# Queries of two tiles in one product, key sums as a column of the key-value product, epsilon on VectorE, the first key weights in two loads, and a new order: four attention layers on one core

## The chip, the core and the metric

The kernel runs on one core of a Trainium2 chip. TensorE (PE in the profile, with its weight loads as PEld), VectorE (DVE), ScalarE (ACT), GpSimd (POOL) and SyncE (SP, which here only issues transfers) each work through a list of instructions in order and wait for one another through semaphores. The metric is the device time of one execution in microseconds (us); lower is better.

## The reference

A sequence of 2048 rows of 512 numbers (bf16) goes through four layers: A, B, A, B with the same weights for both As and both Bs. Each layer normalises its input, attends with 32 heads of 16 columns, multiplies by an output matrix and adds the result to its input. A is linear attention over the whole sequence, B is softmax attention over a causal window of 256 rows.

```python
def _A_ref(x, wqkv, wo):                      # H = 32 heads, Dh = 16
    qkv = (x @ wqkv).reshape(B, S, 3, H, Dh).transpose(2, 0, 3, 1, 4)
    q, k, v = qkv[0], qkv[1], qkv[2]
    phi = lambda t: jnp.where(t > 0, t + 1, jnp.exp(t)) + 1e-6
    pq, pk = phi(q), phi(k)
    kv = jnp.einsum("bhsd,bhse->bhde", pk, v)
    z = jnp.einsum("bhsd->bhd", pk)
    num = jnp.einsum("bhqd,bhde->bhqe", pq, kv)
    den = jnp.einsum("bhqd,bhd->bhq", pq, z)[..., None] + 1e-6
    return (num / den).transpose(0, 2, 1, 3).reshape(B, S, D) @ wo
def _B_ref(x, wqkv, wo):                      # W = 256
    scores = jnp.einsum("bhqd,bhkd->bhqk", q, k) * (Dh ** -0.5)
    p = _softmax(jnp.where(mask[None, None], scores, -1e9), axis=-1)
    return (jnp.einsum("bhqk,bhkd->bhqd", p, v)).transpose(0, 2, 1, 3).reshape(B, S, D) @ wo
x = x + _A_ref(_layernorm(x), A_wqkv, A_wo); x = x + _B_ref(_layernorm(x), B_wqkv, B_wo)
x = x + _A_ref(_layernorm(x), A_wqkv, A_wo); x = x + _B_ref(_layernorm(x), B_wqkv, B_wo)
```

## The kernel before

The 2048 rows are 16 tiles of 128 rows (`T = 16`), and everything stays in the core's memory: the residual `xres`, the weights, and one array `XQ` that holds, for each tile, first the transposed normalised input, then phi of its queries in the same place, later the queries of B.

The program has five parts. `setup` loads inputs and weights. `layer_a_keys` is the first half of the first A: for each tile it normalises (`norm`), transposes the result into `XQ`, makes the keys (`a_k`: four products 512 columns wide, L420, then phi to `pk`), accumulates `g` (L501) over all tiles, and makes the queries of the tile (`a_q`, through `feat`, L434). `barrier` closes an A: from the key-value sums `kv` and the key sums `z` it makes a masked `pqd` (L543) and `zs` (L544) on VectorE, the combined matrix `M` (products L547), then per group G of four tiles the denominators (`den`, L563), their reciprocals (`rec`, L569), and a product (`spread`, L579) that spreads them over the columns, with which phi of the queries is multiplied in place. `middle` runs a B: per tile j it finishes A's output (`a_out`), normalises, makes queries, keys and values, the scores in slices (L676, L712, L792), exponentials on ScalarE (L686, L721, L801, L754), masks, and the products with the values (L822). `middle(2)` also prepares the second A: for each finished tile `norm`, `a_k`, `a_v` (values to `vA`); `barrier(2)` then has `a_kv` and the queries of the second A; `middle(3)` is the second B. I call the parts phase 1 (the first A's sums), the first B, the crossing (the end of the first B, the second A's sums and its barrier), and the second B.

Queries: `feat` makes a tile's queries in 16 products of 128 columns. Each takes a 128x128 block of `wA` as the weights and the tile's 128 columns of `XQ` as what streams through. `phi` is an exponential on ScalarE (L444, `E`), a clip on VectorE (L447, `E1`) and a maximum on VectorE (L451, `phi`), or, for the tiles in `BY_ACT`, an addition on ScalarE (L446, `R`) and a cheaper maximum (L449, `mx`).

Key-value sums of the second A: `a_kv` does per tile four products of 128 columns (L477) into one PSUM bank and four of one column (L480, keys against a column of ones) into another.

The denominators' epsilon of 1e-6 is a first product of `eps` with ones (four of 32x128 per group) ahead of the sixteen that read `zs`.

The order of all instructions does not come from the code's own order. `place` reads it from `TABLE`, a packed string that names, for all operations, their order, the engine of those that two engines can do, and the PSUM bank of every tile; each engine then runs its part of that order, with waits worked out by `synchronise`.

```python
raw = zlib.decompress(b85decode("".join(TABLE)))
order = [ops[raw[2 * k] + 256 * raw[2 * k + 1]] for k in range(n)]
o.eng = ("PE", "ACT", "DVE", "POOL", "SP")[raw[2 * n + o.i]]
```

Seven products `fill` (L277) and nine at the start (L1082) read zeros and only keep TensorE busy until the first data are there.

## Time and profile before

| | |
|---|---|
| median of 3 runs | 409.82 us (409.52 to 409.96) |
| the profiled execution, its own time | 409.61 us |
| its span from the first to the last instruction | 407.9 us |
| granted TensorE clock in it | 1.00 of full speed |
| PE, DVE, ACT, POOL busy in the span | 385.7, 347.8, 349.4, 131.3 us |

A busy engine is not always the one that sets the time. The profile's chain of waits follows the work that ended last back to the start; a table by stage shows which engine has no idle time in a stage; a row of a group gives count, total and mean length of one kind of instruction. TensorE's products overlap, so the length of one (219 ns for 128 columns) is not what it costs in a row of them; that is read from the chain, where runs of products are merged.

### The profile page before, as it was taken

To read this page: it belongs to the slowest core of one execution; us is meant where nothing else is said; L and a number is where in the kernel's file an instruction comes from. 1 tells how busy PE (TensorE), PEld (TensorE's weight loads), DVE (VectorE), ACT (ScalarE), POOL (GpSimd) and SP (SyncE) were. 2 spreads that over 40 slices of the span, in tenths; PEclk is the share of its full clock that TensorE was granted. 3 is DMA by queue.
4 is the path that set the end of the run, shared out by engine and by line. 5 is a ranking of instruction groups with operands and counts; after the bars stand their busy time and mean duration, and the time that the engine had idled before them with its cause. 6 is when DMAs were issued, how large, how long until landed. Compare 5 with 4: busy or idle time off the path is not lost.

```text
span 407.9 us, 17534 instructions
## 1 busy us (share of the span) xinstructions
PE 385.7 (95%) x7667; PEld 261.3 (64%) x7742; DVE 347.8 (85%) x807; ACT 349.4 (86%) x441; POOL 131.3 (32%) x221
## 2 busy tenths in 40 slices
PE   8999999998999999999999999999999989998996
PEld 3754776776575567565667677686756756666664
DVE  7998899999989999888788779998998688856865
ACT  3753679998999999999997258999999999999992
POOL 5668542211430241432512302230305234510340
PEclk9999999999999999999999999999999999999999
DMA  7567024523354444453232000344315534442551
GB/s 251 117 152 232 15 56 107 119 69 81 80 80 106 71 101 104 92 112 91 56 50 62 14 2 2 102 114 107 94 42 106 90 90 104 81 99 70 136 134 54
DMA packets 66788, 37.19 MB, mean 91 GB/s; under 512 B 47640, under 2 KB 62104, under 8 KB 66712
## 3 DMA queue, kind: packets, MB, share of 16 engines
q1 hardware_dynamic: 66320, 35.02, 36.7%
q8 instruction: 61, 1.00, 1.1%
q0 software_dynamic: 384, 1.05, 0.8%
q14 instruction: 15, 0.12, 0.1%
q10 hardware_dynamic: 8, 0.00, 0.0%
HBM read 6.29 MB, written 2.10 MB: 21 GB/s over the span
## 4 chain that ended last, share of the span: by engine, by line
PE 52%; ACT 31%; DVE 9%; issue 4%; DMA 2%; POOL 1%; POOLq 0%; DVEq 0%
ACT pb L686 20%; PE ps L420 18%; PE ps L434 15%; PE ps L822 6%; ACT vp L686 5%; PE ps L676 4%; PE ps L501 3%; ACT pb L801 3%; DVE stats L374 1%; DVE pb L694 1%; DVE xres L604 1%; ACT tE L444 1%; PE ps L792 1%; DMA XQ<-xn 1%; ACT pb L754 1%
## 5 line engine op out<-in xcount | busy, mean ns | idle before, releaser
L686 ACT ACTIVATE pb<-ps 128x1024 bf16<-128x1024 f32 (+2 forms) x216 | 199.0, 1019 | 6.2 <-PE ps L676 5.3
L822 PEld LDWEIGHTS ps<-vB,pb 128*128 128x128 bf16 x2560 | 79.0, 96 | 13.3 <-DVE pb L694 2.8
L822 PE MATMUL ps<-vB,pb 128*128 128x34 bf16 x2560 | 84.9, 177 | 0.9 <-DVE xn L381 0.5
L434 PE MATMUL ps<-xT,wBp 128*128 128x128 bf16 x1024 | 69.3, 219 | 1.3 <-DMA xT<-xn 0.8
L434 PEld LDWEIGHTS ps<-xT,wBp 128*128 128x128 bf16 x1024 | 58.9, 98 | 13.7 <-issue 4.0
L772 POOL TENSOR_SCALAR_AFFINE_SELECT pb<-pb 128x1024 bf16<-128x1024 bf16 x35 | 40.1, 1145 | 84.2 <-DVE pb L694 33.8
L379 POOL TENSOR_SCALAR ve<-mv 128x1 f32<-128x1 f32 x63 | 16.6, 264 | 149.1 <-DVE mv L375 146.9
L444 ACT ACTIVATE tE<-ps 128x512 bf16<-128x512 f32 x64 | 38.1, 606 | 25.3 <-PE ps L420 12.5
L676 PE MATMUL ps<-XQ,kB 32*128 32x256 bf16 (+3 forms) x992 | 48.0, 267 | 2.9 <-ACT vp L686 0.5
L604 DVE TENSOR_TENSOR xres<-ps,xres 128x512 bf16<-128x512 f32 x63 | 43.0, 684 | 7.3 <-PE ps L420 6.8
L420 PE MATMUL ps<-wA,XQ 128*128 128x512 bf16 x174 | 45.8, 379 | 3.4 <-DMA XQ<-xn 0.9
L694 DVE TENSOR_TENSOR pb<-pb,tri 128x512 bf16<-128x512 bf16 (+1 forms) x108 | 43.6, 417 | 2.7 <-ACT pb L686 2.0
L374 DVE BATCH_NORM_STATS2 stats<-xres 128x6 f32<-128x512 bf16 x64 | 43.5, 683 | 2.5 <-DMA xres<-in_A_x_dram 1.9
L380 POOL TENSOR_TENSOR rs<-ve,negh 128x1 f32<-128x1 f32 x64 | 39.5, 616 | 7.7 <-DVE ve L377 2.4
L801 ACT ACTIVATE pb<-ps 128x1024 bf16<-128x1024 f32 x42 | 41.3, 1058 | 0.5 <-PE ps L792 0.4
L434 PE MATMUL ps<-XQ,wA 128*128 128x128 bf16 x512 | 35.5, 219 | 0.2 <-issue 0.2
L434 PEld LDWEIGHTS ps<-XQ,wA 128*128 128x128 bf16 x512 | 30.8, 98 | 6.6 <-DVE xres L604 0.2
L420 PE MATMUL ps<-wBv,xT 128*128 128x512 bf16 x107 | 30.6, 380 | 2.8 <-issue 1.6
L420 PE MATMUL ps<-M,XQ 128*128 128x512 bf16 x112 | 30.5, 380 | 2.0 <-DVE XQ L591 0.5
L420 PE MATMUL ps<-wBo,oT 128*128 128x512 bf16 x109 | 29.8, 380 | 1.8 <-issue 0.8
L676 PEld LDWEIGHTS ps<-XQ,kB 32*128 32x128 bf16 x992 | 14.9, 92 | 25.7 <-ACT pb L686 8.4
L834 DVE RECIPROCAL rc<-ps 128x16 f32<-128x16 f32 x64 | 16.2, 253 | 14.4 <-PE ps L822 13.9
(126 smaller groups left out, 557.4 us busy)
## 6 DMA issues: line engine op xcount, KB each, us to landing
vB<-vS SPq DMA_DIRECT2D x64, 136.0 KB, 2.5
kB<-vp SPq DMA_DIRECT2D x60, 128.0 KB, 2.2
wA<-in_A_wqkv_dram SPq DMA_DIRECT2D x3, 512.0 KB, 4.5
xres<-in_A_x_dram SPq DMA_DIRECT2D x2, 512.0 KB, 5.6
pb<-in_B_wqkv_dram SPq DMA_DIRECT2D x1, 1024.0 KB, 5.5
out_dram<-xres POOLq DMA_DIRECT2D x8, 128.0 KB, 3.2
out_dram<-xres SPq DMA_DIRECT2D x7, 128.0 KB, 3.0
xres<-in_A_x_dram SPq DMA_DIRECT2D x3, 256.0 KB, 4.8
```

What stands on the lines that cost most here:

```text
L374: self.on("DVE", "stats", lambda e: e.bn_stats(K.stats[:, t, :], x()), key, dve(512), rd=rd, wr=[("stats", t)], **held)
L380: self.pow = self.on("POOL", "pow", lambda e: e.tensor_tensor(K.rs[:, t, :], K.ve[:, t, :], K.negh[:], ALU.pow), key + 0.03, (640, 690), r ...
L420: m = e.matmul(K.ps(ps), lhs(c), rhs(c), start=c == 0 and not whole, stop=c == 3)
L434: m = e.matmul(K.ps(ps)[:, f * P:(f + 1) * P], w(c, f), xT(c), start=c == 0, stop=c == 3)
L444: self.on("ACT", "E", lambda e: e.activation(K.tE[:, s, :], K.ps(ps), ACT.Exp, bias=0.0), key, act(512), wr=[("tE", s)], ps=[ps])
L604: self.on("DVE", "res", lambda e: e.tensor_tensor(K.xres[:, t, :], K.ps(po), K.xres[:, t, :], ALU.add), key, dve(512), rd=[("xres", t)], w ...
L676: m = e.matmul(K.ps(ps[gq])[:, ns * i:ns * i + ns], K.kB[rows, j % 4, 2 * f + b, :, :], K.XQ[rows, f, q:q + ns], start=True, stop=True, ti ...
L686: return e.activation(out(2 * h, 2, ns), i, ACT.Exp, bias=0.0, scale=0.25)
L694: return e.tensor_tensor(x, x, K.tri[:, 0, sh:64].unsqueeze(1).unsqueeze(1).to_broadcast([P, 4, n, 64 - sh]), ALU.mult)
L772: return e.affine_select(out=x, in_=x, compare_op=ALU.is_ge, fill=0.0, base=-2, pattern=[[0, 16], [-2, 64]], channel_multiplier=1)
L801: return e.activation(far(h), i, ACT.Exp, bias=0.0, scale=0.25)
L822: m = e.matmul(K.ps(ps)[:, 34 * u:34 * u + 34], K.P((b // 2) % rp)[:, gq, f, o:o + P], K.vB[:, (b // 2) % 4, b % 2, r, :], start=i == 0, s ...
```

## The change

Four edits and a new table.

**Queries in pairs.** `a_q` is called for two tiles at a time. Each product streams the 256 columns of both tiles past one 128x128 block of weights, so 16 products of 256 columns stand where 32 of 128 stood. The pair fills two PSUM banks, each with half of the features of both tiles. Since phi of the queries overwrites `XQ` of both tiles, the first write waits for all 16 products of the pair (`after=held`).

**Key sums as a 129th column.** Values `vA` now have rows of 516 numbers: four blocks of 128 values, each followed by a one (written by the new `unit`: one memset on VectorE, one on GpSimd). `a_kv` streams 129 columns against the keys, so the last column is the sum of the keys; the one-column products are gone. The operands are swapped, so `barrier(2)` masks two halves on VectorE (`kvm`, `zs`, each twice), transposes on TensorE and copies to `pqd` on VectorE or ScalarE. Phase 1 still has its own sums `z`.

**Epsilon on VectorE.** For groups 1 to 3 the epsilon products are gone, and an addition of 1e-6 to 128x128 numbers in PSUM (`de`) stands ahead of the reciprocal.

**First key weights in two loads.** `wAk` is loaded as two transfers of 256 KB, and each half of a key product waits for its own.

```diff
-        seq += [xs(0, 1), w("wAk", "wA", "A_wqkv", 512, 1024), xs(1, 2), ...
+        def wk(h):
+            return ("wAk%d" % h, lambda e: e.dma_start(K.wA[:, 2 * h:2 * h + 2, 512:1024], ...), 262144, [("wAk", h)])
+        seq += [xs(0, 1), wk(0), wk(1), xs(1, 2), ...
...
-    def a_q(self, t, key, near=False):
-        ps = self.feat("q", t, lambda c, f: K.wA[:, c, f * P:(f + 1) * P], lambda c: K.XQ[:, c, t * P:(t + 1) * P], [("XQ", t), ("wAq",)], key)
-        self.phi(ps, lambda: K.XQ[:, :, t * P:(t + 1) * P], [("XQ", t)], key + 0.1, 1, near)
+    def a_q(self, u, keys, near):
+        own = [("XQ", 2 * u), ("XQ", 2 * u + 1)]
+        wide = lambda t: slice(256 * (t // 2), 256 * (t // 2) + 256)
+        for t in (2 * u, 2 * u + 1):
+            ps = Tile(1, K.cls)
+            xT = lambda c, t=t: K.XQ[:, c, wide(t)]
+            for h in range(2):
+                def put(e, h=h, t=t, ps=ps, xT=xT):
+                    f = 2 * (t % 2) + h
+                    for c in range(4):
+                        m = e.matmul(K.ps(ps)[:, 256 * h:256 * h + 256], K.wA[:, c, f * P:(f + 1) * P], xT(c), start=c == 0, stop=c == 3)
+                self.pe("q", put, keys[t % 2] - 0.001 * h, 4, 256, rd=own + [("wAq",)], ps=[ps])
+        held = [o for x in own for o in self.g.r[x]]
+        for t in (2 * u, 2 * u + 1):
+            d = t % 2
+            out = lambda t=t: K.XQ[:, 2 * (t % 2):2 * (t % 2) + 2, wide(t)]
+            wr = [("XQ2", 2 * u), ("XQ2", 2 * u + 1)] if d else own
+            self.phi(tiles[d], out, wr, keys[d] + 0.1, 1, t in near, after=held)
...
+    def unit(self, a, b, more, key):
+        x = lambda: K.vA[:, a:b, :].rearrange("p t (f x) -> p t f x", f=4)[:, :, :, P:P + 1]
+        self.g.add("unit", {"POOL": (300, 360), "DVE": dve(4 * (b - a))}, lambda e, eng: e.memset(x(), 1.0), ...)
...
-                e.matmul(K.ps(kv)[:, fs], K.vA[:, t, fs], K.pk[:, t, fs], ...)
-                m = e.matmul(K.ps(z)[:, f:f + 1], K.pk[:, t, fs], K.ones[:, 0:1], ...)
+                m = e.matmul(K.ps((kv, z)[f // 2])[:, 129 * (f % 2):129 * (f % 2) + 129], K.pk[:, t, f * P:(f + 1) * P], K.vA[:, t, 129 * f:129 * f + 129], ...)
...
+        if late:
+            for h, x in enumerate((kv, z)):
+                self.on("DVE", "kvm", lambda e, h=h, two=two: e.tensor_tensor(K.oT[:, 0, 2 * h:2 * h + 2, :], two()[:, :, 0:P], ...
+                self.on("DVE", "zs", lambda e, h=h, two=two: e.tensor_tensor(K.zs[:, 2 * h:2 * h + 2, :], ...
+            self.transpose("T", lambda: K.oT[:, 0, :, :].rearrange("p f n -> p (f n)"), lambda: K.pqd[:], ..., True)
...
-                for i in range(5):
+                for i in range(1 if G else 0, 5):
...
+            if G:
+                self.on("DVE", "de", lambda e, ps=ps: e.tensor_scalar(K.ps(ps)[:, 0:P], K.ps(ps)[:, 0:P], 1e-6, None, op0=ALU.add), k + 0.05, dve(128), ps=[ps])
...
 TABLE = (
-    r"c-qZ(1Jo_cu5~4qq^h=U+qP}nwr$(CZQHhO+qTZ@{=U8ccX95y=VH9^_Zq8_N@kLoRMzScDx?aflnSfDsqiX-LPaW}N~992Br2l%>b|&dE|SWsvZ<shvij^k",
+    r"c-qZb1DGz$uB}v(O4V%Jwr$(CZQHhO+qP}nwr#!s|JnP!bI-ZH=eytQnVzn$N>;6`q%(idC>2(PQ{hzz6;g##p;ZKhidAeCN5xg~R73^J1Oy4-fJiE<%BJEg",
...
+ROW = D + 4
...
-            sb("vp", [2 * T, D]); ...
+            sb("vp", [T * (ROW + D)]); ...
```

The new table changes the order on every engine. Two places of it matter below; before and after print the lines of their own source (L434 is L483 after, L547 is L581, L563 is L597, L686 is L723).

The first place is TensorE in the crossing, from the last key-value products to `M`. Before:

```order
L477 MATMUL ps<-vp 128x128 x4
L480 MATMUL ps<-ones,vp 128x1 x4
L434 MATMUL ps<-XQ,wA 128x128 x8
L563 MATMUL ps<-ones,eps 32x128 x4
L563 MATMUL ps<-XQ,zs 32x128 x16
L434 MATMUL ps<-XQ,wA 128x128 x8
L547 MATMUL ps<-wAo,pqd 128x512 x3
L579 MATMUL ps<-rec,spread 128x128 x16
```

And now:

```order
L506 MATMUL ps<-vp 128x129 x24
L483 MATMUL ps<-XQ,wA 128x256 x8
L398 MATMUL ps<-ident,oT 128x128 x4
L597 MATMUL ps<-ones,eps 32x128 x4
L597 MATMUL ps<-XQ,zs 32x128 x16
L581 MATMUL ps<-wAo,pqd 128x512 x2
L483 MATMUL ps<-XQ,wA 128x256 x4
L581 MATMUL ps<-wAo,pqd 128x512
L616 MATMUL ps<-rec,spread 128x128 x16
```

The transposes of the masked sums (L398, `ident,oT`) are new, and no queries stand between the denominators and `M` any more.

The second place is ScalarE at the start of the first B, where the exponentials of the scores (L721 and L686 before, L758 and L723 after) begin. L444 and L447 are the `E` of phi, L407 and L410 copies out of PSUM, L627 and L664 the copy of keys. Before:

```order
L627 ACTIVATE vp<-ps 128x512
L721 ACTIVATE pb<-ps 128x8x128 x4
L407 ACTIVATE XQ<-ps 128x4x128
L444 ACTIVATE tE<-ps 128x512
L627 ACTIVATE vp<-ps 128x512
L686 ACTIVATE pb<-ps 128x2x2x256 x10
L444 ACTIVATE tE<-ps 128x512
L627 ACTIVATE vp<-ps 128x512
L686 ACTIVATE pb<-ps 128x2x2x256 x8
```

And now:

```order
L664 ACTIVATE vp<-ps 128x512
L758 ACTIVATE pb<-ps 128x8x128 x4
L410 ACTIVATE XQ<-ps 128x4x128
L447 ACTIVATE tE<-ps 128x512
L664 ACTIVATE vp<-ps 128x512
L723 ACTIVATE pb<-ps 128x2x2x256 x18
```

An `E` and a copy of keys have left the run of exponentials; the eighteen now follow one another.

More of the change, by code (lines that the diff above doesn't have):

```diff
@@ L437, in feat, with phi @@
         return ps
-    def phi(self, ps, out, wr, key, ring, near=False):
+    def phi(self, ps, out, wr, key, ring, near=False, after=()):
         K = self
@@ L450, in phi @@
         else:
-            self.on("DVE", "phi", lambda e: e.scalar_tensor_tensor(out(), view(K.ps(ps)), 1.0 + 1e-6, view(K.tE[:, s, :]), ALU.add, ALU.max), key + 0.02, dve(512), rd=[("tE", s)], wr=wr, ps=[ps])
+            self.on("DVE", "phi", lambda e: e.scalar_tensor_tensor(out(), view(K.ps(ps)), 1.0 + 1e-6, view(K.tE[:, s, :]), ALU.add, ALU.max), key + 0.02, dve(512), rd=[("tE", s)], wr=wr, ps=[ps], after=after)
     def a_k(self, t, key):
@@ L475, in put @@
             for f in range(4):
-                fs = slice(f * P, (f + 1) * P)
-                e.matmul(K.ps(kv)[:, fs], K.vA[:, t, fs], K.pk[:, t, fs], start=t == 0 and f == 0, stop=t == T - 1, skip_group_check=True)
-            for f in range(4):
-                fs = slice(f * P, (f + 1) * P)
-                m = e.matmul(K.ps(z)[:, f:f + 1], K.pk[:, t, fs], K.ones[:, 0:1], start=t == 0 and f == 0, stop=t == T - 1, skip_group_check=True)
+                m = e.matmul(K.ps((kv, z)[f // 2])[:, 129 * (f % 2):129 * (f % 2) + 129], K.pk[:, t, f * P:(f + 1) * P], K.vA[:, t, 129 * f:129 * f + 129], start=t == 0 and f % 2 == 0, stop=t == T - 1, skip_group_check=True)
             return m
-        self.pe("kv", put, key, 4, 128, occ=330, rd=[("pk", t), ("vA", t), ("ones",)], ps=[kv, z], after=self.closing)
+        self.pe("kv", put, key, 4, 129, rd=[("pk", t), ("vA", t)], ps=[kv, z], after=self.closing)
     def layer_a_keys(self, ph, base):
@@ L907, in middle @@
             self.on("POOL", "zero", lambda e, i=i: e.memset(K.vA[:].rearrange("p t d -> p (t d)")[:, 1152 * i:1152 * i + 1152], 0.0), base - 5, (1080, 1140), wr=self.room[i] + [("vA", 2)])
+        if not last:
+            self.unit(LATE, T, [], base)
         for t in range(min(3, T)):
```

163 lines of the change are left out of this document (89 added, 74 removed).

## The prediction

> **What bounds the kernel now.** I first read the table by stage, cut at the first key products (7 us), the first scores (60), the end of the first B's exponentials (216), the last tile's arrival in the second A (232), the second B's first scores (257) and its last exponentials (397). Columns: stretch, its length, then busy time and instruction count of PE, PEld, DVE, ACT and POOL.
>
> ```profile
> 7.00:60.00 53.00, 52.28 (x569) 32.52 (x576) 49.37 (x122) 30.94 (x54) 33.36 (x65) 1.00 0.48 128
> 60.00:216.00 156.00, 148.66 (x3088) 100.16 (x3121) 140.40 (x325) 151.15 (x177) 44.28 (x73) 1.00 0.40 89
> 216.00:232.00 16.00, 14.93 (x312) 11.31 (x300) 13.03 (x32) 8.49 (x15) 5.32 (x7) 1.00 0.17 36
> 232.00:257.00 25.00, 24.48 (x389) 18.54 (x395) 21.19 (x50) 17.00 (x30) 4.05 (x10) 1.00 0.01 2
> 257.00:397.00 140.00, 132.65 (x3162) 91.40 (x3181) 114.04 (x258) 137.05 (x160) 40.71 (x54) 1.00 0.42 99
> ```
>
> Phase 1 belongs to TensorE (52.28 of 53), the two Bs to ScalarE (151.15 of 156 and 137.05 of 140), and in the crossing TensorE is full again while ScalarE is idle for 7.5 and 8.0 us. The chain of waits (start, us, what) has these pieces:
>
> ```profile
> 8.15 1.73 PE ps L420 x8
> ...
> 10.10 1.79 PE ps L434 x32
> ...
> 228.03 4.15 DMA XQ<-xn
> ...
> 233.57 0.24 PE ps L477 x4
> 233.82 0.08 PE ps L480 x4
> 233.90 0.24 PE ps L477 x4
> ...
> 240.53 0.39 PE ps L563 x20
> ...
> 241.53 0.59 PE ps L547 x2
> ```
>
> From 7 to 60 us it stays on TensorE; the waits of that engine there, all of them, are
>
> ```profile
> PE ps L420 <- issue: 0.2, 1, 0.2
> PE ps L434 <- issue: 0.2, 1, 0.2
> ```
>
> so phase 1 lasts as long as its products. Outside the Bs and phase 1 the one visible stall is the load at 228.03.
>
> **Phase 1: -0.3 us (0 to -0.6).** The order of the change has the same products ahead of the first scores as before, 176 query products of 128 columns having become 88 of 256. Thirty-two of 128 take 1.79 us, 55.9 ns each; eight of 512 take 1.73 us, 216 ns each. On the line between, 256 columns cost 109 ns, against 112 for two of 128. So the pairs save 88 x 2.5 ns = 0.2 us here, and 256 x 2.5 = 0.6 us in the whole kernel; the bounds are nothing (112) and half of a 512 (108). One group's four epsilon products (a fifth of 0.39 us, 0.08) go too.
>
> The Trainium skill, "TensorE: Matmul & The Clock Gate", section on the back-to-back issue gap, says otherwise: in a sustained stream of weight loads and products, 128 columns cost about 81 ns each, not the isolated 56. The trace does not agree: its stream of 32 runs at 56 with a weight load for each. By the page 512 products would be 41.5 us and halving their number would be worth many times the 0.6; I keep that as a rival below, priced from rows.
>
> The split key load I cost at nothing: TensorE starts its first keys at 6.82 us, and the copy they read ended at 6.70:
>
> ```profile
> 2.27 0.47 SPq L297 DMA_DIRECT2D wA<-in_A_wqkv_dram  x1
> ...
> 6.10 0.60 ACT L402 ACTIVATE XQ<-ps 128x512 bf16<-128x512 bf16 x1 [2.80 <-PE ps L395]
> ...
> 6.82 0.13 PEld L420 LDWEIGHTS ps<-wA,XQ 128*128 128x128 bf16 x2
> ```
>
> The copy hides the weights. The extra issue on SyncE's queue (0.47 us) delays the rows and query weights behind it by that much; TensorE has key products of three tiles (8 x 216 ns and more) ahead of the queries, which cover it. Without that cover it would cost the 0.5 once.
>
> **First B: -1.6 us (0 to -2.0).** This is the new order's part, not one of the four edits. I counted ScalarE's list from the first exponentials of this B to its last: 185 instructions where 188 stood, one `E`, one copy of queries and one copy of keys less. Rows (busy us, mean ns, idle before):
>
> ```profile
> L444 ACT ACTIVATE tE<-ps 128x512 bf16<-128x512 f32 x64 | 38.1, 606 | 25.3 <-PE ps L420 12.5 <-PE ps L434 6.8 <-DVE vp L451 3.8
> ...
> L627 ACT ACTIVATE vp<-ps 128x512 bf16<-128x512 f32 x5 | 4.0, 792 | 0.0
> ```
>
> With the copy of queries as long as the `E` of the same 128x512, 0.606 + 0.606 + 0.792 = 2.0 us go out of the engine that has only 4.85 us of idle time in 156. TensorE's list there is 0.8 us shorter (two products of 512 columns, the epsilons of two groups, 2.5 ns for each of 72 wide products), VectorE's as long as before, with 15.6 us idle. If ScalarE alone decided, all 2.0 would come; if TensorE, 0.8; if the data arrive no earlier, nothing. I take 1.6, since ScalarE has the least room.
>
> **Crossing: -0.4 us (-1.7 to +1.1).** Gone are the one-column products: after the wait that ends at 232.2, eleven tiles of `a_kv` stand on the chain, and row 233.82 shows that one tile's take 0.08 us, 0.10 until the next tile's run at full pace (five tiles more stand ahead of the wait, where they are free): -1.1 us. Streaming 129 columns instead of 128 is under 1 ns a product. The pairs save 44 x 2.5 ns = 0.1.
>
> Added is a longer way from the sums to `M`. The rows for VectorE's part, and two stretches in which VectorE is full (third busy time):
>
> ```profile
> L835 DVE TENSOR_TENSOR o<-ps,rc 128x256 bf16<-128x256 f32 x64 | 26.7, 419 | 1.5
> ...
> L543 DVE TENSOR_TENSOR pqd<-ps,bmask 128x512 bf16<-128x512 f32 x2 | 1.4, 687 | 0.0
> ...
> L544 DVE TENSOR_TENSOR zs<-hot,ps 128x128 bf16<-128x128 bf16 x2 | 0.6, 288 | 1.1 <-PE ps L480 0.6 <-PE ps L524 0.5
> ...
> L377 DVE TENSOR_SCALAR ve<-mv 128x1 f32<-128x1 f32 x1 | 0.2, 154 | 0.0
> ```
>
> ```profile
> 240.00:250.00 10.00, 9.89 (x144) 7.07 (x144) 9.78 (x24) 7.76 (x15) 0.79 (x2) 1.00 0.02 3
> 250.00:260.00 10.00, 9.90 (x183) 7.33 (x182) 9.94 (x24) 9.84 (x15) 2.48 (x6) 1.00 0.15 43
> ```
>
> Before, `zs` and the mask take 0.29 + 0.69. Now two masks of 256 (0.42 each, by L835) and two `zs` of 64 columns (between the 0.15 of one column and the 0.29 of 128; I take 0.22), 1.28 us; then the copy of the transposed sums, between the 0.42 of 256 and the 0.69 of 512 columns from PSUM, taken at the low end, 0.42, since it reads bf16. On TensorE the four transposes take 0.24, as four products of 128 columns do (row 233.57), and wait for both masks: 0.84 plus a hop after the last key-value product, behind eight query products of 0.87, so hardly at all. The denominators, 0.39, run while the copy is made; `M` then follows about 1.85 us after the last key-value product, against 1.46 before (the products ahead of row 240.53 are 8 x 56 ns, so the sums end at 240.07, and `M` starts at 241.53), where sixteen query products fill the time. TensorE thus loses 0.24 + 0.39 = 0.6 us, behind which all queries and the output of the first tiles queue.
>
> `de` is not in the trace: between 0.15 (one column, L377) and 0.29 (128 columns, two operands), taken as 0.22, six times in the kernel. Two of them and the copy fall from 240 on, where VectorE has 0.3 us idle in 20; I count 0.2 of the 0.86 on the path, since TensorE, not VectorE, is the chain there. Sum: -1.1 - 0.1 + 0.6 + 0.2 = -0.4. With VectorE as the bound the additions count whole and the savings not: +1.1. Without the loss of TensorE and with the one-column products of all sixteen tiles on the path: -1.7. ScalarE gets 2.6 us more in the crossing, in 15.5 idle; the ones of `unit` are on queues with room.
>
> **Second B: +0.5 us (0 to +0.8).** The list of exponentials is almost word for word the old one, with one more copy of keys on ScalarE, 0.79 us where 3 are idle in 140. Three `de` meet 26 us idle on VectorE. The end of the kernel has the same products and additions; ten stores instead of eight go over GpSimd's queue, where only the last row's wait counts.
>
> **Sum.** -0.3 - 1.6 - 0.4 + 0.5 = -1.8 us. The profiled execution took 409.61 around its span of 407.9, 0.21 under the median; on the median 409.82 it gives **408.0 us**. My own range for it: all terms at their good ends -4.3, or 405.5; at their bad ends I go up to 409.0.
>
> **Rivals.**
> *Pairs that make phi late: slower.* In the first B a query's `phi` on VectorE could start after its tile's 16 products, 0.89 us; now it waits for the pair's, 1.74, 0.87 later, and masks and the residual queue behind it on VectorE, then the scores' banks, then ScalarE. The first B has 72 of the wide products, 4.5 pairs: 4.5 x 0.87 = 3.9 us if none is hidden. It decides once VectorE reaches the phi less than 0.87 us after the tile's products. For it: VectorE is 90% busy and in order. Against it: 15.6 us idle there. With the other terms: 409.8 - 1.8 + 3.9 = 411.9 us.
> *Shifted rows: slower.* Tiles of `vA` now lie 1032 bytes apart, and eleven transposing loads of phase 1 read them:
>
> ```profile
> XQ<-vp SPq DMA_TRANSPOSE x11, 2.5
> ```
>
> If each took a quarter longer, 0.6 us, and TensorE waited for each, it would be 11 x 0.6 = 6.9; TensorE waited for none before, so I give 2 to 4 of it, 411 us. The Trainium skill, "DMA: Bandwidth & Descriptors", section on how a descriptor splits into AXI transactions, has a transfer that does not start on a 256-byte boundary cost an extra transaction (five for four here); no run here shows it.
> *A new balance that brings nothing.* VectorE is above 90% in the first B and full from 240 to 260, and the work on it grows by 6 x 0.22 + 0.3 + 0.42 = 2 us: the gains of the other two go into its queue, 409.4 us.
> *Weight loads that count.* Were the query products worth their mean busy time,
>
> ```profile
> L434 PE MATMUL ps<-XQ,wA 128*128 128x128 bf16 x512 | 35.5, 219 | 0.2 <-issue 0.2
> ```
>
> that is 35.5 / 512 = 69 ns, the pairs would save 512 x 69 - 256 x 109 = 7.6 us, 402.2 us. Against it: the merged row at 56.
>
> **How the numbers follow.** My forecast has 0.57, the late phi 0.16, the shifted rows 0.05, no change 0.16, the counting weight loads 0.06. What differs by more than 0.2% (0.8 us) from the median can be told from no change here. Faster: forecast and weight loads, 0.63; the same: 0.16; slower: 0.21. The range takes in the good ends and a little of the weight loads, and of the slower cases about half: 404.6 to 411.0.
>
> **What would show it.** In the changed profile: sixteen wide query products in a row last 1.74 us (much less: weight loads count); the first scores start at 59.2 instead of 59.45; ScalarE's busy time in the first B is 2 us less and its stretch as much shorter; `M` starts 1.8 to 1.9 us after the last key-value product; the second B is as long as before plus half a microsecond. Long waits of VectorE's phi for L483, or of TensorE for the transposing loads before 60 us, would prove me wrong, as would idle time of ScalarE within either B.

## The result and the profile after

| | before | changed | ratio (95% interval) |
|---|---|---|---|
| median of 11 runs each, us | 409.74 | 411.29 | 1.0034 (1.0017 to 1.0050) |
| lowest and highest run, us | 409.02, 410.16 | 409.76, 412.84 | |
| profiled execution, us (its span) | 409.61 (407.9) | 412.54 (410.8) | |

The change made the kernel 0.34% slower, about 1.4 us; 408.0 us were predicted, with a range of 404.6 to 411.0. The first B's row of the table by stage, changed kernel, first profile (stretch, length, busy time and count of PE, PEld, DVE, ACT, POOL, granted clock, DMA share, GB/s):

```profile
60.00:216.00 156.00, 147.01 (x2954) 97.53 (x2985) 139.28 (x324) 148.25 (x171) 43.37 (x71) 1.00 0.39 88
```

In the 156 us that held 177 instructions of ScalarE before, 171 now fit: the first B is longer, not shorter. (The 2954 products beside 2985 weight loads are no edit: 31 products left no record, as the second experiment shows for the kernel before.) From the changed kernel's chain of waits (start, us, what), rows at its start, in phase 1 and in the first B:

```profile
5.27 1.28 PE ps L277 x3
...
8.02 0.86 PE ps L423 x4
...
11.05 1.75 PE ps L483 x16
...
134.32 4.05 DMA XQ<-xn
...
138.47 0.41 DVE xn L384
138.88 0.61 DVE XQ L410
...
139.54 0.43 PE ps L616 x16
```

The sixteen wide products take the 1.75 us that I priced. The first key products start at 8.02 (7.01 before), since three fill products still took 1.28 us, 427 ns each, where they took 216 ns each before. In the two traces the first record of the full granted clock is at 7.18 us (changed) and 4.99 us (before). At 134.32 a new wait stands on the chain: the normed rows of the second A have one buffer, VectorE may not write it before the transposing load of the tile before has read it, and a copy of queries, a product and the next factors queue behind. It looked like the cause. By e2 and e6 below it was not: without it the loss stays.

**One table for all runs.** To place gains and losses I counted the 312 exponentials in ScalarE's timeline and split each profiled execution at three of them: number 0 (first scores of the first B), 150 (near its end) and 156 (the second B's first), then the last and the span's end. Worked out from the traces, in us:

```
kernel                          to no. 0  first B  crossing  second B  end   span
before                             59.90   159.18     37.16    142.70  8.93  407.9
before, second profile             59.91   158.95     37.05    142.70  8.93  407.5
changed                            60.46   161.38     35.27    144.11  9.60  410.8
changed, second profile            59.67   160.30     35.27    143.50  9.60  408.3
e1  old code, new order            60.39   160.08     36.77    143.05  9.59  409.9
e2  two xn buffers                 60.47   160.50     35.27    143.86  9.59  409.7
e3  no 129th column                59.74   159.83     36.65    142.84  9.58  408.6
e4  narrow products                61.09   160.96     35.35    145.06  9.60  412.1
e7  before, more ScalarE           60.65   160.97     37.31    142.84  8.93  410.7
e8  before, more TensorE           60.45   162.35     36.74    143.05  8.94  411.5
e9  before, 129th column           59.60   165.69     37.36    142.88  8.94  414.5
e10 mended order                   60.01   161.72     35.27    144.82  9.25  411.1
e11 before, 129th, ones split      59.84   159.26     37.36    144.05  8.98  409.5
e12 before, less ScalarE           60.55   158.56     37.07    142.29  8.93  407.4
e13 old code, new first half       59.88   161.20     38.96    142.68  9.42  412.1
e14 old code, new second half      60.13   158.95     40.59    143.64  9.58  412.9
e15 changed, old end               59.54   161.42     35.27    143.81  8.94  409.0
e16 e15 with two xn buffers        60.22   160.46     35.27    144.33  8.94  409.2
```

The first column varies from 59.5 to 60.7 with either code (e4 apart): what the first profile lost there is not the change's. The second profiles of the two kernels differ by 0.8 us of span, and the stretches add up to it: -0.24 + 1.35 - 1.78 + 0.80 + 0.67 = 0.80.

### The profile page after: what moved, and what is told of

Its sections match the earlier page's. It is cut to its first block, busy times and chain, and to the rows that moved or that the text cites. A ratio compares the mean times of both kernels' runs of the same rounds, so it can differ in the third digit from the quotient of the medians.

```text
span 410.8 us, 16888 instructions
## 1 busy us (share of the span) xinstructions
PE 385.4 (94%) x7327; PEld 256.1 (62%) x7402; DVE 345.7 (84%) x814; ACT 351.1 (85%) x444; POOL 132.5 (32%) x224
## 4 chain that ended last, share of the span: by engine, by line
PE 67%; ACT 13%; DVE 11%; issue 5%; DMA 4%; POOL 1%; POOLq 0%; DVEq 0%
PE ps L423 22%; PE ps L437 11%; PE ps L859 11%; ACT pb L723 8%; PE ps L713 6%; PE ps L483 6%; PE ps L527 3%; ACT vp L723 3%; DMA XQ<-xn 2%; DMA oT<-o 2%; DVE xres L641 2%; PE ps L829 2%; DVE XQ L628 1%; DVE stats L377 1%; PE ps L1124 1%
## 5 line engine op out<-in xcount | busy, mean ns | idle before, releaser
L723 ACT ACTIVATE pb<-ps 128x1024 bf16<-128x1024 f32 (+2 forms) x216 | 199.5, 1024 | 8.3 <-PE ps L713 7.7
L447 ACT ACTIVATE tE<-ps 128x512 bf16<-128x512 f32 x64 | 37.9, 604 | 18.9 <-PE ps L423 9.9
L731 DVE TENSOR_TENSOR pb<-pb,tri 128x512 bf16<-128x512 bf16 (+1 forms) x108 | 42.3, 402 | 3.7 <-ACT pb L723 3.6
L383 POOL TENSOR_TENSOR rs<-ve,negh 128x1 f32<-128x1 f32 x64 | 38.2, 596 | 7.5 <-DVE ve L380 2.3
L483 PE MATMUL ps<-XQ,wA 128*128 128x256 bf16 x256 | 33.5, 273 | 0.9 <-ACT pb L723 0.4
L423 PE MATMUL ps<-wBo,oT 128*128 128x512 bf16 x103 | 28.2, 380 | 3.9 <-DMA oT<-o 1.3
L483 PEld LDWEIGHTS ps<-XQ,wA 128*128 128x128 bf16 x256 | 23.6, 98 | 8.2 <-ACT pb L723 0.9
```

The lines of the kernel that those rows point to most:

```text
L383: self.pow = self.on("POOL", "pow", lambda e: e.tensor_tensor(K.rs[:, t, :], K.ve[:, t, :], K.negh[:], ALU.pow), key + 0.03, (640, 690), r ...
L423: m = e.matmul(K.ps(ps), lhs(c), rhs(c), start=c == 0 and not whole, stop=c == 3)
L483: m = e.matmul(K.ps(ps)[:, 256 * h:256 * h + 256], K.wA[:, c, f * P:(f + 1) * P], xT(c), start=c == 0, stop=c == 3)
L723: return e.activation(out(2 * h, 2, ns), i, ACT.Exp, bias=0.0, scale=0.25)
L731: return e.tensor_tensor(x, x, K.tri[:, 0, sh:64].unsqueeze(1).unsqueeze(1).to_broadcast([P, 4, n, 64 - sh]), ALU.mult)
```

## The experiments

The theories: **A**, the new order loses the time and the four edits are worth about their price, in its narrow form by single new waits; **B**, pairs of queries come late; **C**, the waits only show where work piles up; **D**, TensorE and not ScalarE bounds the Bs. Ratios are to the kernel before, run on the same chip.

### The order alone: e1, old code in the new order

```diff
-    TABLE of before (order, engines, banks)
+    TABLE of the changed kernel, without the 14 operations that only it has
```

> The kernel before, instruction for instruction (query products of one tile, key sums by one-column products, epsilon by TensorE, one load of key weights), put in the order, on the engines and in the PSUM banks of the changed kernel's table. Theory A (the new order loses the time, the four edits are worth about what I priced them at): 411 to 412 us, with VectorE waiting 1 to 2 us for the transposing load ahead of a second A's xn between 130 and 150 us, and the exponential number 78 about 1.3 us later than in the kernel before. Rival B (the queries of two tiles do it: a pair's phi comes late): no loss in this kernel, 408 to 409.8 us, and no such wait.

Measured: 411.75 us, 1.0062 (1.0043 to 1.0082). The order alone loses 2.5 us by the ratio; the edits in it (1.0034) give about 1.1 back, though the two intervals overlap. B falls: this kernel has no pairs, and in e6 VectorE's phi of queries waits only 0.3 us for the products of a pair in the whole first B. The wait that I had named is not in e1's profile (number 78 comes 0.8 us later than in e5, but 72 was already 0.7 late, 0.5 of it from the start), so A holds and its narrow form is in doubt. The split load and the epsilon on VectorE have no run of their own.

### What bounds the Bs: e5, e7, e8, e12

The prediction rests on ScalarE's being the fuller engine. The first row of the page for before, then the same row of its second profile:

```profile
PE 385.7 (95%) x7667; PEld 261.3 (64%) x7742; DVE 347.8 (85%) x807; ACT 349.4 (86%) x441; POOL 131.3 (32%) x221
```

```profile
PE 394.2 (97%) x7742; PEld 262.0 (64%) x7742; DVE 347.3 (85%) x807; ACT 349.2 (86%) x441; POOL 131.4 (32%) x221
```

e5 is the kernel before, unchanged.

> The kernel before, unchanged, for a second profile: the first one has 7667 products beside 7742 weight loads of TensorE, so 75 products, all of 512 columns, left no record. Theory D (TensorE bounds the whole kernel, and the idle time that I read for it in the two Bs is made of missing records): with all records TensorE's busy time is 394 to 396 us instead of 385.7, and in the first B (60 to 216 us) it is idle for under 3 us, less than ScalarE's 4.9. The reading of the prediction (ScalarE bounds the Bs): 7 us idle of TensorE in the first B stay.

With all records TensorE is busy for 394.2 us, 8.5 more, and by the table by stage of this second profile idle for 2.6 us of the first B, less than ScalarE (4.7):

```profile
60.00:216.00 156.00, 153.43 (x3125) 100.43 (x3123) 140.63 (x325) 151.27 (x177) 44.34 (x73) 1.00 0.41 89
```

The page had said so: each product has its weight load, and 7667 stand beside 7742. D's numbers hold (TensorE's busy time has modelled ends in it, so its 2.6 us of idle time are an estimate). Both engines are nearly full there, and the next three runs load or relieve one of them.

```diff
 e7:  e.activation(K.tE[:, s, :], K.ps(ps), Exp)
+     ahead of it: e.activation(K.pqd half, K.ps(ps)[:, 0:256], Exp)        (13 tiles)
 e8:  for c in (2 * h, 2 * h + 1): e.matmul(K.ps(ps), lhs(c), rhs(c), ...)
+     ahead of it, twice: e.matmul(K.ps(ps), lhs(0), rhs(0), start, stop)    (11 tiles)
-e12: e.activation(K.tE[:, s, :], K.ps(ps), Exp)
+e12: e.activation(K.tE[:, s, 0:64], K.ps(ps)[:, 0:64], Exp)                 (8 tiles)
```

> The kernel before with twelve more activations of 128x256 on ScalarE in the first B (each exponent of a second A key tile, 2 to 13, is taken once more of half its columns, into the free buffer pqd): 12 x 0.38 = 4.6 us of work, each right ahead of the E that VectorE waits for. ScalarE bounds the Bs (the prediction's reading, 4.9 us idle in 156): 3 us or more slower. Theory D (TensorE bounds them): 0 to 1.5 us slower.

> The kernel before with 22 more products of 512 columns on TensorE in the first B (two ahead of the value products of tiles 1 to 11, overwritten by them): 22 x 0.216 = 4.75 us of work. ScalarE bounds the Bs (7.3 us idle of TensorE in 156): 0 to 2 us slower. Theory D: 4 to 5 us slower.

> The kernel before with less work on ScalarE in the first B: the exponents of eight key tiles of the second A (2 to 9) are taken of 64 columns instead of 512, the other columns keep what stood there. From 0.60 us for 512 columns and 0.38 for 256 about 0.21 for 64, so 8 x 0.39 = 3.1 us less work; TensorE and VectorE have the same work. The prediction's term (1.6 of 2.0 us saved on ScalarE come out): 407.2 us. The rate of the run with more work on ScalarE (2.2 us for 4.6): 408.2 us. If TensorE sets the first B: 409.3 to 409.7.

The totals of the three profiles, e7, e8 and e12:

```profile
PE 395.8 (96%) x7742; PEld 262.2 (64%) x7742; DVE 347.8 (85%) x807; ACT 352.5 (86%) x454; POOL 131.5 (32%) x221
```

```profile
PE 399.5 (97%) x7764; PEld 264.3 (64%) x7764; DVE 348.0 (85%) x807; ACT 350.3 (85%) x441; POOL 131.2 (32%) x221
```

```profile
PE 394.7 (97%) x7742; PEld 262.2 (64%) x7742; DVE 347.1 (85%) x807; ACT 346.7 (85%) x441; POOL 131.4 (32%) x221
```

Measured: e7 1.0053 (1.0037 to 1.0068), so 3.3 us more of ScalarE cost 2.2; e8 1.0087 (1.0067 to 1.0107), 5.3 us more of TensorE cost 3.6; e12 0.9983 (0.9973 to 0.9992), 2.5 us less of ScalarE give 0.7. The edit of e7 takes thirteen tiles, not the twelve of the expectation (454 instructions of ScalarE where 441 stood). Work added to either engine costs two thirds of itself, but work taken from ScalarE returned a quarter: by the intervals 0.46 to 0.84 of what was added in e7 and 0.13 to 0.44 of what was taken in e12. The quarter may be too much: e12's profile has 0.4 us of its gain in the first B and 0.4 in the second, where nothing was edited. That TensorE holds the rest fits these numbers; VectorE, busy for 140.63 of the 156 us, was never loaded or relieved by itself, so its part isn't known. This is the number that the prediction lacked. Neither reading was right as it stood: ScalarE does not bound the first B alone, and neither does TensorE.

### The changed kernel again: e6

> The changed kernel, unchanged, for a second profile and more times. If the 1.1 us that its first profile lost between the exponentials number 72 and 78 (VectorE waiting for a transposing load that took 4.05 us) were the order's doing, they are lost here too; if that was one slow load, the exponential number 78 comes 0.2 to 0.7 us later than in the kernel before, and the profiled time is 410 to 411.5 us. Under both, the parts that four kernels in this order lose alike stay: 1.4 us gained between number 12 and 18, 1.8 lost between 24 and 42, 2.1 lost between 180 and 186.

Measured over ten runs: 411.51 us, 1.0036 (1.0020 to 1.0051), its profiled execution 410.07. The loss of 1.1 us between the exponentials 72 and 78 is not in it; e13 and e15 have it (1.0 and 1.4 us) and e4 a part (0.6), e1, e3 and e10 don't (0.1 to 0.2). There a load is just in time or just not. The gain between 12 and 24 and the loss between 24 and 42 and between 180 and 186 are in every profile that has the new order there.

### The waits: e2, e10, e16

```diff
 e2, e16:
-    self.norm(j, k, 3, ...)            # the one xn buffer
+    self.norm(j, k, 3 + j % 2, ...)    # slot 4 is pqd
```

> The changed kernel with one edit: the normed rows of the second A alternate between their one buffer and the buffer pqd, which is free from 60 to 240 us, so that VectorE's next xn needn't wait until the transposing load of the tile before has read the only buffer. Order, engines and banks as they were. Theory A in its narrow form (this wait starts the loss of the first B): VectorE's waits for that load are gone, the exponential number 78 comes 1.0 to 1.3 us earlier, and the kernel takes 409.3 to 410.3 us. Rival C (TensorE and VectorE are full there, the wait only shows where work piles up): the wait goes, but the scores come no earlier, 411 us and more.

Measured: 411.14 us, 1.0042 (1.0027 to 1.0057). The wait is gone and so is the jump at 72 to 78 (which e6 lacks too, with one buffer), but not the loss: that is what C expects. I then mended four places at which the chain of the second profile leaves TensorE's work. This is the worst of them (e6's chain of waits):

```profile
203.18 1.83 PE ps L423 x8
205.01 0.36 PE ps L713 x8
...
205.39 1.95 ACT pb L723 x2
...
207.39 1.05 PE ps L483 x8
208.44 0.33 PE ps L713 x8
```

Query products wait until ScalarE has read two tiles of scores, since their bank held scores, and the next scores stand behind them. In e10 they go behind those scores; the other moves, in TensorE's order:

```diff
 L713 MATMUL ps<-XQ,kB 128x256 x8
-L423 MATMUL ps<-wBo,oT 128x512 x2
 L423 MATMUL ps<-wA,XQ 128x512 x4
+L423 MATMUL ps<-wBo,oT 128x512 x2
 L829 MATMUL ps<-XQ,kB 128x64 x32
...
 L713 MATMUL ps<-XQ,kB 128x256 x8
-L423 MATMUL ps<-wA,XQ 128x512 x4
 L859 MATMUL ps<-vB,pb 128x34 x48
+L423 MATMUL ps<-wA,XQ 128x512 x4
...
-L483 MATMUL ps<-XQ,wA 128x256 x8
 L713 MATMUL ps<-XQ,kB 128x256 x8
+L483 MATMUL ps<-XQ,wA 128x256 x8
...
+L423 MATMUL ps<-wBo,oT 128x512 x2
 L859 MATMUL ps<-vB,pb 128x34 x24
 L713 MATMUL ps<-XQ,kB 128x64 x8
-L423 MATMUL ps<-wBo,oT 128x512 x2
```

> The changed kernel with four places of its order put as they were before, or past a wait, nothing else: the query products that wait for a bank of scores go behind the next scores (with the first half's phi), two output products of the first B go behind the key products of A instead of waiting for their transposing load, key products that wait for their load go behind value products of B, and the last but two output products go ahead of the last scores, their load and bank with them. Theory A (the order's loss is made of such places, at which TensorE waits for a bank or a load while ScalarE runs dry): 0.5 to 0.8 us at the exponentials 132 to 144, 0.2 to 0.5 at each of the two loads, 0.4 to 0.6 behind the last exponential, 1.2 to 2 us in all: 409.5 to 410.3 us. If the loss is spread over the order (TensorE's work moved out of stretches that ScalarE bounds into stretches that TensorE bounds): the waits go, but most of the time stays, 411 us.

Measured: 412.85 us, 1.0070 (1.0049 to 1.0090), slower than the changed kernel. Beside e6, the two moves at the loads gained 0.5 us (exponentials 102 to 108) and lost 1.0 behind it (108 to 114), the one at the scores lost 0.8 (138 to 144), and the last made the end 0.3 shorter and the last exponential 0.7 later. Gains at the places that were mended came with losses elsewhere. A's narrow form falls, at least for these four places together; no run moves one of them alone. e16 comes from e15 (below):

> The changed kernel with the old end (from some 294 us on) and with the second xn buffer of the second A (pqd). If the wait for the one buffer explains the spread: the exponential number 78 is no more than 0.3 us behind the number 72 in its distance to the kernel before, and the times are 409.3 to 410.3 us with their median at 409.8, no slower than before. If it is one of several loads that come late now and then: 410.3 to 410.7 us, as with one buffer, and a spread of 1.5 us or more.

Measured: 410.76 us, 1.0028 (1.0011 to 1.0045), from 409.84 to 413.76. The second buffer doesn't narrow the spread, so this wait does not explain it.

### The 129th column: e3, e9, e11

```diff
 e3, in the changed kernel:
-    m = e.matmul(K.ps((kv, z)[f // 2])[:, 129 columns], pk, vA[:, t, 129 * f:129 * f + 129], ...)
+    e.matmul(K.ps(kv)[:, fs], K.vA[:, t, fs], K.pk[:, t, fs], ...)
+    m = e.matmul(K.ps(z)[:, f:f + 1], K.pk[:, t, fs], K.ones[:, 0:1], ...)
 e9, in the kernel before, in its own order: the reverse, with the ones and the transposes
 e11:
-    self.unit(0, LATE, ...)
+    self.unit(0, 2, ...)               # ahead of the values of tile 0
+    self.unit(2, LATE, ...)            # ahead of those of tile 4
```

> The changed kernel with the key sums of the second A by one-column products again (64 of them, ones as the moving operand), and so without the ones in the rows, without the transposes of the sums and their copy, with one mask and one zs; all else in the new order. By my terms the 129th column is worth -1.1 + 0.6 + 0.1 (the copy's part) = -0.4 us, so 411.5 to 412.0 us and M about 1.5 us after the last key-value product; if the longer way from the sums to M costs more than it saves, 410.3 to 411.0 us.

> The kernel before, in its own order, with one of the four edits: the key sums of the second A as the 129th column (rows of 516 elements, the ones, two masks and two zs, the transposes of the sums and their copy). Three kernels with the 129th column take 35.2 to 35.3 us from the first B's last exponentials to the second B's first, two without it 36.6 and 36.8, so the edit is worth 1.4 us of the crossing: 408.3 us (407.9 to 408.7), faster than both kernels. By my own price for the edit alone (-1.1 + 0.6 + 0.1 = -0.4 us) it would be 409.3 us.

> The kernel before, in its own order, with the 129th column, as in the run that took 417.5 us, but the ones for the last five tiles of values are written in two pieces, each right ahead of the values that need it. In that run one memset waited 2.4 us on VectorE for the last copy of keys out of the same rows (which landed at 202.8 us), with the copies of other values behind it, and TensorE and ScalarE behind those: 6.6 us between the exponentials 126 and 138. If that wait was all of it, no stretch of the first B is longer than before and the crossing shows what the 129th column is worth: 408.3 us if 1.4, 409.3 if 0.4.

Measured: e3 412.33 us, 1.0079 (1.0050 to 1.0108), with a crossing of 36.65 against 35.27; e9 417.55, 1.0188 (1.0166 to 1.0210); e11 411.23, 1.0027 (1.0012 to 1.0043), with a crossing of 37.36 against 37.05. So in single profiles the column is worth 1.4 us of the crossing in the new order and costs 0.3 in the old one. The chains of waits of the crossing say why, first before (second profile), then the changed kernel (e6):

```profile
227.81 4.04 DMA XQ<-xn
...
231.90 1.04 PE ps L420 x4
```

```profile
232.12 1.18 PE ps L506 x20
233.30 0.86 PE ps L423 x4
234.16 0.22 PE ps L398 x4
234.39 2.59 PE ps L423 x12
236.98 1.42 PE ps L506 x24
238.40 0.87 PE ps L483 x8
239.27 0.39 PE ps L398 x4
...
239.68 0.44 DVE pqd L405
...
240.16 0.61 PE ps L581 x2
```

Before, TensorE waits in the crossing for the last tiles' load, and the one-column products of the tiles ahead of it are free. In the new order nothing is waited for, every product counts, and the longer way to `M` (1.76 us from the last key-value product, 238.40, to 240.16) is filled with eight query products and the transposes.

e9 shows what a wait in the wrong place costs. Its chain of waits:

```profile
200.61 2.17 DMA kB<-vp
...
202.90 0.09 DVE vp L474
...
203.01 0.70 DVE vp L407
...
203.85 0.42 PE ps L685 x8
...
204.30 1.95 ACT pb L695 x2
```

A memset of 0.09 us (L474, the ones) stood ahead of a copy of values on VectorE and waited for the last copy of keys out of the same rows; the first B grew by 6.7 us. Not all of that is the wait. 4.2 us of it come between the exponentials 126 and 132, where TensorE stands still, and 1.9 between 132 and 138, where the granted clock (third number from the end) is at half for 3.4 us and four products of 512 columns take 1.89 us, 472 ns each, instead of 216. The same stretch of half clock stands at the end of e11. Rows of the tables by stage, e9 and then e11:

```profile
206.00:209.36 3.36, 3.07 (x14) 0.85 (x15) 1.14 (x2) 1.74 (x3) 0.00 (x0) 0.50 0.02 4
```

```profile
397.90:401.30 3.40, 3.40 (x85) 2.52 (x85) 1.51 (x5) 2.19 (x5) 0.00 (x0) 0.50 0.13 43
```

Split and moved (e11), the first B is 0.3 longer than before; most of the rest of e11's loss is in its last exponentials: 0.8 us up to number 306, where TensorE waited 0.6 us for a copy of values that came late, and 0.7 behind it, in the half clock. In the new order the last copy of keys is issued at 196.0 us (e6) and not at 200.8 (e5), so the memset meets no such wait there; whether the new order pays for that at other places was not shown.

### The pairs: e4

```diff
-    m = e.matmul(K.ps(ps)[:, 256 * h:256 * h + 256], w, xT(c), ...)
+    for v in range(2): m = e.matmul(K.ps(ps)[:, cs:cs + P], w, xT(c)[:, v * P:v * P + P], ...)
```

> The changed kernel with each query product of 256 columns as two of 128 (512 instead of 256 in all), into the same places, in the same order, with the same waits. By my price (2.5 ns for each of 256) it is 0.6 us slower, 411.9 us, with 32 products of 128 in 1.79 us where 16 of 256 take 1.75; if the weight loads count in the two Bs and the crossing though they don't in phase 1, 3 us or more slower.

Measured: 413.63 us, 1.0087 (1.0068 to 1.0107), 2 us over the changed kernel. The products themselves have the price that I gave: in phase 1, from one start to the next, 176 narrow ones take 9.87 us (56 ns each) and 88 wide ones 9.68 (110 ns). That is 2.2 ns for each wide one, some 0.6 us in the kernel; where the other 1.4 us go, its profile doesn't settle (the second B is 145.06, 1.0 to 1.6 above the changed kernel's two), and it stays open. The Trainium skill, "TensorE: Matmul & The Clock Gate", section on the back-to-back issue gap, has some 81 ns for 128 columns in a stream; these 56 don't agree.

### The halves of the order and its end: e13, e14, e15

```diff
 e13: order, engines, banks: new up to the end of the first B's exponentials, old from there (code of before)
 e14: old up to there, new from there (code of before)
 e15: the changed kernel; from some 294 us on the old order, engines and banks
```

> The code of before; order, engines and banks of the changed kernel's table up to the end of the first B, of its own table from there on. If the order's loss lies in the first B (159.0 us from first to last exponential before, 160.1 in the new order): about 1.1 us slower than before, 410.8 us. If it lies in the rest: 409.5 to 409.9. With the prediction's reading (2.0 us less of ScalarE's list in the first B): 408 us.

> The code of before; its own order up to the end of the first B, and the changed kernel's from there on. The rest of the order loses, by single profiles, 0.4 to 0.8 us in the second B and 0.65 behind the last exponential, and gains 0.3 in the crossing: 410.5 to 410.9 us. If the first B had all of the loss: 409.5 to 409.9.

> The changed kernel up to the last queries of the second B (some 294 us), from there on the order, engines and banks of the table of before. If the end of the new order is a loss of its own (0.65 us from the last exponential to the end in five profiles): 410.6 to 411.0 us. If the end only shows what comes late anyway: 411.3 to 411.5.

Measured: e13 413.49 us, 1.0090 (1.0071 to 1.0109); e14 413.60, 1.0087 (1.0065 to 1.0108); e15 410.68, 1.0020 (1.0011 to 1.0030). The sums of the two halves are no use, since the seam costs 1.9 and 3.5 us of crossing. In e14 a part of that is again a stretch of half clock:

```profile
229.20:232.60 3.40, 3.40 (x25) 2.08 (x23) 0.00 (x0) 1.19 (x2) 0.00 (x0) 0.50 0.19 39
```

The stretches outside the seam are of use: with the same code the first B takes 161.20 us (e13) or 160.08 (e1) in the new order and 158.95 to 159.18 in the old, the second 143.64 (e14) or 143.05 (e1) in the new and 142.68 to 142.70 in the old. e15's end is 8.94 us instead of 9.60, and by the ratios the kernel is faster than the changed one by about 0.6 us (their intervals overlap; the stretch is plain); it is the best version of the changed code that I found, and none beats the kernel before.

At the end one move can be pointed at, though no run isolates it. TensorE's timeline (start, us, operation), before (second profile) and changed (e6):

```profile
396.91 0.61 PE L420 MATMUL ps<-wBo,oT 128*128 128x512 bf16 x2
397.35 0.76 PE L822 MATMUL ps<-vB,pb 128*128 128x34 bf16 x24
398.04 0.24 PE L676 MATMUL ps<-XQ,kB 32*128 32x64 bf16 x8
```

```profile
396.94 0.77 PE L859 MATMUL ps<-vB,pb 128*128 128x34 bf16 x24
...
398.18 0.24 PE L713 MATMUL ps<-XQ,kB 32*128 32x64 bf16 x7 [0.27 <-issue]
398.35 0.60 PE L423 MATMUL ps<-wBo,oT 128*128 128x512 bf16 x2
```

Two output products stood ahead of the last scores and now follow them. e15 puts back the whole order from 294 us on and has the old end. e10 puts back these two products alone at the end: there the end is 0.3 us shorter, and the last exponential 0.7 later. So the move is at most a part of it.

### Where the first B goes longer

With the same code, stretches between the same exponentials in e5 (old order), then in e1 (new order); the first row of each is the whole first B, the others the numbers 12 to 24, 24 to 42 and 42 to 72:

```profile
59.91:218.86 158.95, 156.38 (x3193) 102.75 (x3192) 142.51 (x330) 153.45 (x180) 45.04 (x74) 1.00 0.40 88
73.30:86.35 13.05, 13.05 (x280) 10.03 (x277) 11.79 (x31) 12.82 (x17) 2.89 (x6) 1.00 0.45 103
86.35:107.51 21.16, 20.36 (x451) 14.28 (x449) 20.72 (x48) 19.53 (x25) 4.04 (x7) 1.00 0.31 73
107.51:136.85 29.34, 28.33 (x636) 18.75 (x635) 26.89 (x66) 29.21 (x35) 9.73 (x17) 1.00 0.48 90
```

```profile
60.39:220.47 160.08, 157.31 (x3194) 102.64 (x3193) 141.98 (x329) 152.62 (x178) 43.10 (x71) 1.00 0.41 88
74.23:85.57 11.34, 11.32 (x246) 8.07 (x241) 10.39 (x27) 11.27 (x14) 1.60 (x4) 1.00 0.48 88
85.57:108.60 23.03, 22.70 (x485) 16.30 (x484) 22.08 (x52) 21.23 (x27) 4.02 (x7) 1.00 0.35 80
108.60:137.53 28.93, 27.53 (x629) 18.27 (x628) 25.94 (x65) 28.93 (x34) 10.39 (x18) 1.00 0.41 90
```

Where TensorE is full the length follows what was put there: 34 products fewer, 1.7 us shorter; 34 more, 1.9 longer. These rows don't single out TensorE, though: in the first of the two stretches ScalarE is nearly as full (12.82 of 13.05 and 11.27 of 11.34) and loses 1.6 us of work, in the second VectorE is as full (20.72 of 21.16 and 22.08 of 23.03) and gets 1.4 more. Where ScalarE is full (29.21 of 29.34 and 28.93 of 28.93) 0.8 us less of TensorE and 0.3 less of ScalarE bring 0.4. Over the whole first B ScalarE has 0.8 us less work, TensorE's count is the same and its busy time 0.9 more, and the stretch is 1.1 longer. Since a product's end is modelled, short waits can hide in that busy time. Which waits they are, beyond the three of e10 in the first B, stays open; mending those three together did not bring the time back.

## Why the prediction was wrong, step by step

**What bounds the first B: wrong, and the step that failed.** "ScalarE has the least room" came from 4.85 us of idle time of ScalarE beside 7.3 of TensorE, and the 7.3 were mostly missing records (2.6 with all of them). The term that hangs on it is -1.6 us for 2.0 fewer on ScalarE. It failed in three ways. At the quarter that e12 measured, 2.0 us would be worth about -0.5. Of the 2.0, only 0.9 left the stretch up to number 150 (153.45 us busy in e5, 152.57 in e6), 1.6 up to the last exponential of this B. And the term took for granted, without a reason, that the rest of the new order costs nothing there; e1 shows that it costs 1.1 us of the first B with the old code. The first B became 1.4 us longer in the second profile, 2.2 in the first. e6's row of the whole first B, beside that of e5 above:

```profile
59.67:219.97 160.30, 156.90 (x3125) 101.62 (x3124) 142.37 (x332) 152.57 (x178) 43.22 (x72) 1.00 0.40 88
```

ScalarE's idle time in it grew from 5.5 to 7.7 us, one of the signs that the prediction had named for its being wrong.

**Phase 1: right.** From the first key product to the first exponential it took 52.80 us before (e5) and 52.57 after (e6): -0.2, with -0.3 predicted, and most other profiles agree (52.80 to 52.85 in four of six of the old code and order, 52.57 to 52.65 in five of six of the changed one). The split load cost nothing that shows. "First scores at 59.2" missed because the first key product starts anywhere between 6.7 and 7.9 us, with either code.

**Crossing: the good end of its bounds came true, the size was off.** -1.8 measured, -0.4 predicted, with -1.7 for the case that all sixteen tiles count and the longer way is hidden. I counted the one-column products of eleven tiles, because five stood ahead of a wait; the new order has no such wait, so all sixteen count (64 products, 1.66 us in e1), and the 0.6 and 0.2 us that I charged for the longer way and VectorE's extras are hidden, although `M` starts 1.76 us after the last key-value product, nearly the 1.85 that I gave. By the profiles of e1 and e3 the order alone has 0.3 of the 1.8, the column 1.4. One detail went against me: 129 columns take 59 ns (24 in 1.42 us), not "under 1 ns" more than the 55 to 56 of 128.

**Second B: +0.8 and +1.4 measured, +0.5 predicted**, in the two profiles; no run separates the copy of keys and the additions that I charged there, and e1, which lacks the additions, has +0.3. **The end** I priced at nothing ("the same products and additions"); it cost 0.7. I had looked at what is in the list, not at what stands ahead of the last scores.

**The range.** The bad ends of the four terms add up to +1.9 us, 411.7; I wrote "up to 409.0" without a reason, and 411.0 with the rivals. The measured 411.29 lies between the two.

**The rivals.** The late phi of pairs, which I gave 0.16 and 411.9 us, would have been near the time for the wrong reason: e1 has no pairs and loses more. Shifted rows show no cost; the changed profile's issues have the same median:

```profile
XQ<-vp SPq DMA_TRANSPOSE x11, 2.5
```

The counting weight loads fall by e4's products. "A new balance that brings nothing" was nearest; that VectorE, which I named, is the engine was neither shown nor excluded.

## What to carry to other kernels

Compare the counts of products and weight loads before reading an engine's idle time off a profile: one per cent of missing records turned the fuller of two engines into the emptier one. Where two engines are both nearly full, price a saving on one of them by what the other still has to do in the same stretch: here it returned a quarter. A new order is an edit with a price of its own: run the old code in it, before pricing what else was changed. Before a longer stretch is put down to a wait alone, read the granted clock there.

## What the runs showed that I had not expected

Work added to either engine in the first B cost 0.66 to 0.68 of itself and work taken from one returned 0.28; the two directions are not alike.

The start of the first key product varied by 1.2 us between executions (6.7 to 7.9). The fill products ahead of it take 427 ns each until the trace's first record of the full clock and 216 behind it; that record is at 3.9 to 7.3 us, with either code, and where it is late (6.8 to 7.3) the first key product is too (7.6 to 7.9).

The granted clock also fell to half for 3.41 us within three profiles: at 205.95 us in e9, 229.18 in e14 and 397.91 in e11. One such stretch makes a mean clock of 0.996. The kernel before had 0.998 or more in each of the 91 executions that ran beside the experiments; the changed kernel had 0.995 or 0.996 in four of 21. Without these four its medians are 411.1 us (ten executions) and 411.5 (seven), so the loss does not come from them. Why the clock falls in some executions and not in others was not worked out.

And the kernels in the new order, or with the 129th column, have times that spread over 1.5 to 5 us; those of the kernel before, on the same chips, over 1.1 to 2.9. In the first B, transposing loads stand on the chain of waits in ten of the thirteen profiles of the former and in none of the five of the old order without the column. That these make the spread was not shown: taking one of them away left 1.5 us in e2 and 3.9 in e16.
